# Two borders from attention to feed-forward: the order of LayerNorm, queries and transposes

## The chip, the cores and the metric

The kernel runs on one core of one Trainium2 chip. The time is the device time of one execution in microseconds (us). Engines are named as the profile names them: PE (TensorE), DVE (VectorE), ACT (ScalarE), POOL (GpSimd), SP (here the queue that issues every DMA). Each engine works through its own instructions in the order in which the program gives them; semaphores tie the engines together.

## The reference, cut to what matters

A network of four layers, attention A, feed-forward B, A, B, on one sequence of 2048 tokens of width 512, and the gradients of its input and of all weights. Every layer normalises its input without learned scale and is added back to it.

```python
def _A_ref(x, wqkv, wo):            # 32 heads of 16, linear attention
    q, k, v = split(x @ wqkv)
    phi = lambda t: jnp.where(t > 0, t + 1, jnp.exp(t)) + 1e-6
    pq, pk = phi(q), phi(k)
    kv = jnp.einsum("bhsd,bhse->bhde", pk, v)
    z = jnp.einsum("bhsd->bhd", pk)
    num = jnp.einsum("bhqd,bhde->bhqe", pq, kv)
    den = jnp.einsum("bhqd,bhd->bhq", pq, z)[..., None] + 1e-6
    return merge_heads(num / den) @ wo

def _B_ref(x, w_gate, w_up, w_down):
    return (sigmoid(x @ w_gate) * (x @ w_up)) @ w_down

x = x + _A_ref(_layernorm(x), A_wqkv, A_wo)      # layer 0
x = x + _B_ref(_layernorm(x), ...)               # layer 1
x = x + _A_ref(_layernorm(x), A_wqkv, A_wo)      # layer 2
x = x + _B_ref(_layernorm(x), ...)               # layer 3
# outputs: x and its vector-Jacobian product with grad_out
```

## The kernel before

The sequence is cut into 16 tiles of 128 tokens (`st`). The forward part takes about the first 430 us, the backward part the rest. All order is written out by hand: on each engine, instructions run as the Python emits them.

**Attention, `kq_fwd` (layers 0 and 2).** A loop over the 16 tiles projects keys and queries (`proj`, L604, four 128x512 matmuls each, in PSUM banks that rotate over "t", "t", "y"), takes the exponential on ACT (L621), and finishes phi on DVE with a clamp (L624) and `phi_out` (L627). The sum X = h^T phi(k) grows in four PSUM banks (L612); `X_some` emits XSTEP = 4 of its 64 matmuls per tile from tile 2 on. The queries of the last QLATE = 2 tiles, 14 and 15, are left for behind the loop: `late_q` emits the matmuls ("t_mm") and the exponential, and returns a function that does the clamp, `phi_out` and the store.

Behind the loop comes the border. X is copied out by ACT (L750), multiplied with the value weights (`kv_ps`, L758), masked (`kvbdT`, L760) and multiplied with wo (`M_ps`, L765); M turns normalised queries into the layer's output. For each tile, `prod` multiplies phi(q) by the sum z (DVE for tiles 0 and 1, POOL after that, L815), `front1` reduces it to the denominator (L821), `front2` adds epsilon, inverts and writes the normalised queries "pqn" (L831, L832, L833), `front3` transposes them on PE into the bank "ln" (L355) and copies them out on ACT (L364, "pqnT"). `attn_mm` multiplies by M (`y_ps`, L854), `attn_add` adds the residual (L862) and takes the LayerNorm statistics (bn_stats L448, aggregate L450 on DVE, three small POOL instructions L451, L452, L454). `ln.apply` normalises on ACT (L459), `stage_T` transposes that in the same bank "ln" and copies it out on DVE ("hT"). "ln" and "y" are single PSUM banks; "t", "g" and "u" have two buffers.

**Feed-forward, `ab_fwd` (layers 1 and 3).** For each tile, `gu` makes gate and up products of one of three column slices (L909, eight matmuls), two sigmoids on ACT (L911, L913), their product with up on DVE (`hh`, L914) and one more product on POOL (L915). `transposes(T, fs)` turns a slice around in a bank "t" (L923) and copies it out on ACT (L926). `finish` multiplies by w_down in bank "y" (L935) and adds on DVE (L937). The fronts of attention run FLAG = 3 tiles ahead inside this loop, so the first tile of feed-forward overlaps the last steps of the border. `fill` emits weight transposes, one group per "t" bank ("wT_ps", L390 in layer 1, L416 and L433 in layer 3); `fill.share` spreads the groups left evenly over the tiles left, and 16 groups are to be placed in layer 1, 34 in layer 3. `A.extra` holds the copy of a group whose transposes were emitted earlier. `early_T` transposes the first two tiles of the next attention layer, between layers 1 and 2.

The order that the change touches, before it, in the border:

```python
        A.front1(1)
        A.attn_y(0)
        A.front2(1)
        phis = [late_q(st) for st in range(NST - QLATE, NST)]
```

Of the kernel before, what the change touches and what calls it, by code (L numbers as in the profile page):

```python
# [23 lines left out]
NST = S // P  # L24
# [334 lines left out]
def evac_copy(k, dst, src, evac):  # L359
    nc = k.nc  # L360
    if evac == "vector":
        nc.vector.tensor_copy(dst, src)  # L362
    elif evac == "scalar":
        nc.scalar.copy(dst, src)  # L364
    else:
        nc.any.tensor_copy(dst, src)
# [183 lines left out]
XSTEP = 4  # L550
# [5 lines left out]
def kq_fwd(k, aq, l, ln, ln_next, x_src=None):  # L556
# [10 lines left out]
    with ExitStack() as ctx:  # L567
# [47 lines left out]
        def X_some(n, upto):  # L615
            while n > 0 and Xq and Xq[0][0] <= upto:
                X_mm(*Xq.pop(0))
                n -= 1
# [36 lines left out]
        def late_q(st):  # L655
            ps = proj(st, 0, ps_tile(k, "t", [P, D], F32, "t_mm"))
            e_t, a_t = qa_tiles()
            exp_to(e_t, ps)

            def phi():  # L660
                clamp(a_t, e_t)
                phi_out(A.pq_all[:, st, :], ps, a_t)
                save_phq(st, a_t)
            return phi
# [17 lines left out]
        for st in range(NST):  # L682
            if st == 2:
                X_ps += [ps_tile(k, "gu"[i % 2], [P, D], F32, "X_ps") for i in range(NDC)]
            both = st < NST - QLATE
            ps_k = proj(st, 1)
            if l == 0:
                e_t = work.tile([P, 2, D], BF16, name="e_t", bufs=2)
                a_t = work.tile([P, 2, D], BF16, name="a_t", bufs=3)
                ek, ak, eq, aqt = e_t[:, 0, :], a_t[:, 0, :], e_t[:, 1, :], a_t[:, 1, :]  # L690
            else:
                ek = work.tile([P, D], BF16, name="e_t", bufs=4)[:]
                ak = work.tile([P, D], BF16, name="ak_t", bufs=1)[:]
            exp_to(ek, ps_k)
            if l == 0 and st < 2:
                stage_hT([2 * st + 1], "scalar" if st else "vector")
            elif l == 2 and st == 0:
                stage_hT([2, 3], "vector")
            elif st % 2 == 1 and st >= 3:
                stage_hT([st + 1, st + 2], "vector" if l == 2 and st % 4 == 1 else "scalar")  # L700
            if l == 2 or not both:
                clamp(ak, ek)
                phi_out(pk_all[:, st, :], ps_k, ak)
            if both:
                ps_q = proj(st, 0, ps_tile(k, "u", [P, D], F32, "u_mm") if st == 1 else None)
                if l == 2:
                    eq, aqt = qa_tiles()
                exp_to(eq, ps_q)
            if l == 0:
                if st == 0:  # L710
                    stage_hT([2], "scalar")
                if st == 2:
                    ln.apply(4)
                if st != 1:
                    ln.apply(st + 3)
                if both:
                    clamp(a_t[:], e_t[:])
                    phi_out(pk_all[:, st, :], ps_k, ak)
            elif st in (1, 2):
                ln.apply(NST - 3 + st)  # L720
            if both:
                if l == 2:
                    clamp(aqt, eq)
                phi_out(A.pq_all[:, st, :], ps_q, aqt)
                save_phq(st, aqt)
            if l == 0:
                if st == 0:
                    ln.stats(4)
                ln.stats(st + 5)
            z_sum(st - ZLAG)  # L730
            store_pk(st)
            X_some(XSTEP, st - 2)

        z_ps = mm_tile()
        nc.tensor.matmul(z_ps[:], lhsT=k.ones32[:], rhs=zs, start=True, stop=False)
# [12 lines left out]
        for ic in range(NDC):  # L748
            X_mm(NST - 1, ic)
            nc.scalar.copy(X_sb[:, ic, :], X_ps[ic][:])  # L750
        nc.sync.dma_start(out=sv["X"].rearrange("(c p) j -> p c j", p=P), in_=X_sb[:])

        kv_ps = ps_tile(k, "y", [P, D], F32, "kv_ps")
        kv3 = kv_ps[:].rearrange("p (c f) -> p c f", c=NDC)
# [8 lines left out]
        for c in range(NDC):  # L763
            m_ps = ps_tile(k, "gu"[c % 2], [P, D], F32, "M_ps")
            nc.tensor.matmul(m_ps[:], lhsT=kvbdT[:, c, :], rhs=k.wo[:, c, :], start=True, stop=True)  # L765
            evac_copy(k, A.M_sb[:, c, :], m_ps[:], "vector" if c % 2 else "scalar")
        A.front1(1)
        A.attn_y(0)
        A.front2(1)
        phis = [late_q(st) for st in range(NST - QLATE, NST)]  # L770
        nc.scalar.activation(k.tab[:], k.neg[:], ACT.Sigmoid)
        mt_ps = []
        for jc in range(NDC):
            mt_ps.append(ps_tile(k, "gu"[jc % 2], [P, D], F32, "M_ps"))
            for c in range(NDC):
                nc.tensor.matmul(mt_ps[jc][:, c * P:(c + 1) * P], lhsT=k.wo[:, c, jc * P:(jc + 1) * P],
                                 rhs=kvbdT[:, c, :], start=True, stop=True)
        A.front3(1)
        phis[0]()
        A.ln.apply(0)  # L780
        for jc in range(NDC):
            nc.scalar.copy(MT_sb[:, jc, :], mt_ps[jc][:])
        nc.sync.dma_start(out=sv["MT"].rearrange("(c p) j -> p c j", p=P), in_=MT_sb[:])
        A.attn_mm(1)
        phis[1]()
    k.kv[l] = dict(kvbdT=kvbdT, zb=A.zb, rden_all=A.rden_all)

    def tail(fill):
        fill("tt", "vector")
        A.ln.stage_T(0)  # L790
        A.prod(2)
        A.prod(3)
        A.attn_add(1)
        A.front1(2)
        A.front2(2)
        A.extra = fill.mm("t")
    A.tail = tail
    return A
# [93 lines left out]
def ab_fwd(k, A, ln, fill, nxt=None, out_cb=None, last_cb=None):  # L892
# [3 lines left out]
    with ExitStack() as ctx:  # L896
# [20 lines left out]
        def transposes(T, fs):  # L917
            hh_t, hhT = T["hh"], T["hhT"]
            fcs = fchunks_of_slice(fs)
            tps = ps_tile(k, "t", [P, 8, P], BF16, "t_tp")  # L920
            for i, fc in enumerate(fcs):
                r = fc_rows(fc)
                nc.tensor.transpose(tps[0:r, i, :], hh_t[:, fc * P:fc * P + r], k.ident[:])  # L923
            nfull = len([fc for fc in fcs if fc_rows(fc) == P])
            if nfull > 0:
                nc.scalar.copy(hhT[:, fcs[0]:fcs[0] + nfull, :], tps[:, 0:nfull, :])  # L926
            if nfull < len(fcs):
                nc.scalar.copy(hhT[0:FLAST, NFC - 1, :], tps[0:FLAST, nfull, :])
# [21 lines left out]
        for st in range(NST):  # L950
            hT = ln.pop(st)
            T = dict(st=st,
                     ssd=wide.tile([P, 2, F], BF16, name="ssd_t"),
                     hh=wide.tile([P, F], BF16, name="hh_t"),
                     hhT=wide.tile([P, NFC, P], BF16, name="hhT"))
            nfill = fill.share(st)
            if st == 0:
                gu(T, hT, 0)
                A.extra("vector")
                A.front1(FLAG)  # L960
                A.front3(2)
                ln.apply(1)
                gu(T, hT, 1)
                transposes(T, 0)
                A.attn_y(2)
                ln.stage_T(1)
                gu(T, hT, 2)
                A.front2(FLAG)
            else:
                A.prod(st + FLAG)  # L970
                gu(T, hT, 0)
                if st == 1:
                    A.front3(FLAG)
                else:
                    A.attn_y(st + YLAG)
                after(st - 2)
                if nfill > 0:
                    fill("t", "vector")
                gu(T, hT, 1)
                if st == 1:  # L980
                    A.attn_y(FLAG)
                transposes(T, 0)
                ln.stage_T(st + 1)
                A.front1(st + FLAG)
                gu(T, hT, 2)
                A.front2(st + FLAG)
            if l == 1 and st == NST - 1:
                nc.scalar.activation(k.tab[:], k.neg[:], ACT.Exp)
            transposes(T, 1)
            ln.apply(st + YLAG)  # L990
            if st == NST - 1:
                if last_cb is not None:
                    last_cb(0)
                if nxt is not None:
                    nxt.early_T()
            if st == 0:
                fill("t", "vector")
            if prev is not None:
                finish(prev)
            if st > 0:  # L1000
                A.front3(st + FLAG)
            if st > 0 and nfill > 1:
                fill("t" * (nfill - 1), "scalar" if st % 2 else "vector")
            transposes(T, 2)
            nc.sync.dma_start(out=sv["ssd"][rows(st), :, :], in_=T["ssd"][:])
            nc.sync.dma_start(out=sv["hdd"][0, :, :, st, :].rearrange("g p w -> p g w"),
                              in_=T["hh"][:, 0:NG * GW].rearrange("p (g w) -> p g w", g=NG))
            nc.sync.dma_start(out=sv["hdl"][0, :, st, :], in_=T["hh"][:, NG * GW:F])
            prev = T
        if out_cb is not None:  # L1010
            out_cb(NST - 2)
        if last_cb is not None:
            last_cb(1)
        finish(prev)
        if out_cb is not None:
            out_cb(NST - 1)
# [747 lines left out]
```

## Time and profile before

| | |
|---|---|
| median of 3 runs | 1202.06 us (1201.79 to 1202.13) |
| the profiled execution | 1202.16 us |
| its span in the trace | 1200.4 us |
| PE busy in the span | 1169.6 us (97%) |
| DVE, ACT, POOL busy | 730.6, 593.2, 290.2 us |
| granted PE clock | 1.00 |
| DMA, mean | 213 GB/s |

A row of the timeline gives start and length in us, engine, line, operation, tiles (written <- read), shape and count; in brackets stands how long the engine had been idle before it and what ended that. Several instructions of one line in a row are merged ("x8"). A matmul's end is modelled, and the matmuls of a row overlap, so the idle time in brackets is a little shorter than the room that one more instruction would find. The list of waits adds up such idle time by who waited for whom. "issue" is time for which the profile shows no releaser. Lines are those of the code above.

### The profile page before, as it was taken

To read this page: it belongs to the slowest core of one execution; us is meant where nothing else is said; L and a number is where in the kernel's file an instruction comes from. 1 tells how busy PE (TensorE), PEld (TensorE's weight loads), DVE (VectorE), ACT (ScalarE), POOL (GpSimd) and SP (SyncE) were. 2 spreads that over 40 slices of the span, in tenths; PEclk is the share of its full clock that TensorE was granted. 3 is DMA by queue.
4 is the path that set the end of the run, shared out by engine and by line. 5 is a ranking of instruction groups with operands and counts; after the bars stand their busy time and mean duration, and the time that the engine had idled before them with its cause. 6 is when DMAs were issued, how large, how long until landed. Compare 5 with 4: busy or idle time off the path is not lost.

```text
span 1200.4 us, 21734 instructions
## 1 busy us (share of the span) xinstructions
PE 1169.6 (97%) x8185; PEld 717.5 (60%) x8302; DVE 730.6 (61%) x1414; ACT 593.2 (49%) x1100; POOL 290.2 (24%) x498
## 2 busy tenths in 40 slices
PE   8989999998999999999999999999999999999998
PEld 4445555444555555555546568865556745547887
DVE  6788886777777556665884760056664976751111
ACT  6667776547766644444635641144444625630010
POOL 5646665425666410000110010000100110110000
PEclk9999999999999999999999999999999999999999
DMA  8834455434546777977765859558897685749874
GB/s 263 290 136 156 168 180 183 154 137 165 188 149 232 237 228 249 336 217 222 239 190 165 263 172 315 136 161 261 256 298 224 207 275 164 231 117 350 258 208 151
DMA packets 266233, 256.05 MB, mean 213 GB/s; under 512 B 43280, under 2 KB 251024, under 8 KB 261264
## 3 DMA queue, kind: packets, MB, share of 16 engines
q1 hardware_dynamic: 266128, 254.65, 66.5%
q8 instruction: 65, 1.06, 0.4%
q14 instruction: 40, 0.33, 0.1%
HBM read 135.69 MB, written 118.92 MB: 212 GB/s over the span
## 4 chain that ended last, share of the span: by engine, by line
PE 92%; DVE 4%; ACT 2%; issue 1%; DMA 1%; another core or an unknown queue 0%; SPq 0%; ACTq 0%; DVEq 0%
PE p_ps L1408 17%; PE dh_ps L1174 13%; PE dh_ps L1622 7%; PE p_ps L1394 6%; PE dhh_ps L1059 6%; PE u_ps L909 6%; PE g_ps L909 6%; PE y_ps L935 6%; PE T_ps L1134 3%; PE GT_ps L1535 2%; PE y_ps L854 2%; PE dp_ps L1510 2%; PE dpk_ps L1653 2%; PE t_mm L604 2%; PE t_tp L923 2%; PE X_ps L612 1%
## 5 line engine op out<-in xcount | busy, mean ns | idle before, releaser
L1408 PE MATMUL p_ps<-p_set,p_a 128*128 128x256 bf16 (+1 forms) x2048 | 211.7, 264 | 0.6 <-DVE dw_stg L1384 0.5
L1408 PEld LDWEIGHTS <-p_a 128*128 128x128 bf16 x2048 | 185.9, 98 | 22.5 <-issue 0.7
L1067 DVE TENSOR_TENSOR dd<-dhh_ps,ssd 128x512 bf16<-128x512 f32 x144 | 82.5, 629 | 136.7 <-PE dhh_ps L1059 131.8
L1138 ACT COPY ddT<-T_ps 128x1024 bf16<-128x1024 bf16 (+1 forms) x96 | 83.0, 867 | 124.7 <-PE T_ps L1134 124.3
L1033 POOL TENSOR_SCALAR ab<-c 128x2 f32<-128x2 f32 x64 | 12.3, 192 | 436.4 <-DVE junk L1030 405.1
L915 POOL TENSOR_TENSOR ssd_t<-hh_t,oms 128x512 bf16<-128x512 bf16 (+1 forms) x96 | 101.7, 1064 | 55.5 <-ACT out_t L219 41.1
L1174 PEld LDWEIGHTS <-ddT 128*128 128x128 bf16 (+1 forms) x704 | 67.7, 98 | 69.3
L909 PEld LDWEIGHTS <-hT 128*128 128x128 bf16 x768 | 71.1, 98 | 56.6 <-DVE hT L362 1.0
L1384 DVE TENSOR_TENSOR dw_stg<-p_ps,dw_stg 128x512 bf16<-128x512 f32 (+3 forms) x44 | 28.5, 649 | 109.4 <-PE p_ps L1408 84.2
L909 PE MATMUL g_ps<-wg,hT 128*128 128x512 bf16 (+1 forms) x381 | 89.6, 357 | 0.8 <-DVE hT L362 0.6
L909 PE MATMUL u_ps<-wu,hT 128*128 128x512 bf16 (+1 forms) x384 | 90.0, 357 | 0.0
L914 DVE TENSOR_TENSOR hh_t<-u_ps,ssd_t 128x512 bf16<-128x512 f32 (+1 forms) x96 | 61.0, 636 | 45.9 <-PE u_ps L909 24.5
L1174 PE MATMUL dh_ps<-wgT,ddT 128*128 128x512 bf16 (+1 forms) x352 | 86.2, 379 | 0.0
L1174 PE MATMUL dh_ps<-wuT,ddT 128*128 128x512 bf16 (+1 forms) x351 | 81.2, 379 | 0.1
L1394 PE MATMUL p_ps<-p_a,p_set 128*128 128x512 bf16 (+1 forms) x343 | 79.9, 379 | 0.5
L1025 ACT ACTIVATE t_sb<-dh_ps,rstd_all 128x512 f32<-128x512 f32 x64 | 44.0, 687 | 71.2 <-issue 38.4
L1059 PE MATMUL dhh_ps<-wdT,gT 128*128 128x512 bf16 (+1 forms) x341 | 75.8, 355 | 2.1 <-DVE dd L1067 0.5
L935 PE MATMUL y_ps<-wd,hhT 128*128 128x512 bf16 (+1 forms) x322 | 75.1, 379 | 2.2 <-DVE x L937 0.6
L1030 DVE SCALAR_TENSOR_TENSOR junk<-t_sb,h_ld 128x512 bf16<-128x512 f32 x64 | 44.0, 688 | 48.7 <-ACT t_sb L1025 46.9
L911 ACT ACTIVATE ssd_t<-g_ps 128x512 bf16<-128x512 f32 (+1 forms) x96 | 53.2, 554 | 30.8 <-PE g_ps L909 30.6
L1386 ACT CAST dw_stg<-p_ps 128x512 bf16<-128x512 f32 (+2 forms) x43 | 24.1, 560 | 67.8 <-PE p_ps L1408 61.1
L1394 PEld LDWEIGHTS <-p_set 128*128 128x128 bf16 (+1 forms) x352 | 33.6, 100 | 34.9
(239 smaller groups left out, 2158.4 us busy)
## 6 DMA issues: line engine op xcount, KB each, us to landing
p_set<-sv_hdd SPq DMA_DIRECT2D x30, 1024.0 KB, 6.4
sv_ssd<-ssd_t SPq DMA_DIRECT2D x32, 688.0 KB, 3.4
ssd<-sv_ssd SPq DMA_DIRECT2D x24, 688.0 KB, 5.2
sv_hdd<-dd SPq DMA_DIRECT2D x48, 320.0 KB, 3.6
sv_hdd<-hh_t SPq DMA_DIRECT2D x32, 320.0 KB, 2.6
h_ld<-sv_h SPq DMA_DIRECT2D x32, 256.0 KB, 5.1
p_a<-sv_h SPq DMA_DIRECT2D x16, 512.0 KB, 6.2
p_set<-sv_dqk SPq DMA_DIRECT2D x8, 1024.0 KB, 7.9
```

The costliest lines, as they stand in the source:

```text
L909: nc.tensor.matmul(ps[:, 0:w], lhsT=hT[:, kc, :], rhs=w_sb[:, kc, c0:c0 + w], start=(kc == 0), stop=(kc == NDC - 1))
L911: nc.scalar.activation(ssd_t[:, 0, c0:c0 + w], g_ps[:, 0:w], ACT.Sigmoid)
L914: nc.vector.tensor_tensor(hh_t[:, c0:c0 + w], u_ps[:, 0:w], ssd_t[:, 0, c0:c0 + w], ALU.mult)
L915: nc.gpsimd.tensor_tensor(ssd_t[:, 1, c0:c0 + w], hh_t[:, c0:c0 + w], oms[:, 0:w], ALU.mult)
L935: nc.tensor.matmul(y_ps[:], lhsT=T["hhT"][0:r, fc, :], rhs=k.wd[0:r, fc, :], start=(fc == 0), stop=(fc == NFC - 1))
L1059: k.nc.tensor.matmul(ps[:, 0:w], lhsT=gT[:, jc, :], rhs=k.wdT[:, jc, c0:c0 + w], start=(jc == 0), stop=(jc == NDC - 1))
L1067: k.nc.vector.tensor_tensor(dd[:, a, c0:c0 + w], ps[:, 0:w], ssd[:, a, c0:c0 + w], ALU.mult)
L1138: nc.scalar.copy(ddT[:, :, f0:f0 + nfull, :], tps[:, :, 0:nfull, :])
L1174: nc.tensor.matmul(T["dh"][:], lhsT=ddT_block(T, a, fc), rhs=(k.wuT, k.wgT)[a][0:r, fc, :], start=(i == 0), stop=(i == 2 * NFC - 1))
L1394: nc.tensor.matmul(ps[0:r, :], lhsT=set_t[:, st, c * P:c * P + r], rhs=self.ops[j["l"], "g"][:, st, :], start=(st == 0), stop=(st == NST - 1))
L1408: nc.tensor.matmul(ps[:, icl * w:(icl + 1) * w], lhsT=self.ops[j["l"], "h"][:, st, ic * P:(ic + 1) * P], rhs=set_t[:, st, 0:w], start=(st ...
L1622: nc.tensor.matmul(dh_ps[:], lhsT=lhsT, rhs=rhs, start=(i == 0), stop=(i == len(ops) - 1))
```

## The change

In `kq_fwd`, behind the loop: the queries of tile 14 are projected ahead of `kv_ps` and not behind y(0); y(0) with its add and statistics stands ahead of `front1(1)`; `front3(1)` stands behind `ln.apply(0)`; `stage_T(0)` stands ahead of `attn_mm(1)`. `tail` keeps one weight-transpose group of three, and gives `front2(2)` to the feed-forward loop. In the first tile there, `front3(2)` and y(2) come one slice later, the extra group's copy goes to ACT, two fill groups stand where one stood, and the last transposes of tile 0 move into tile 1. One X matmul of tile 2 is left for later. `early_T` moves behind the last tile's transposes.

```diff
-            X_some(XSTEP, st - 2)
+            X_some(XSTEP - (st == 2), st - 2)
...
             nc.scalar.copy(X_sb[:, ic, :], X_ps[ic][:])
         nc.sync.dma_start(out=sv["X"].rearrange("(c p) j -> p c j", p=P), in_=X_sb[:])
+        phis = [late_q(NST - 2)]
...
+        A.attn_y(0)
         A.front1(1)
-        A.attn_y(0)
         A.front2(1)
-        phis = [late_q(st) for st in range(NST - QLATE, NST)]
+        phis.append(late_q(NST - 1))
         nc.scalar.activation(k.tab[:], k.neg[:], ACT.Sigmoid)
...
-        A.front3(1)
         phis[0]()
         A.ln.apply(0)
+        A.front3(1)
         for jc in range(NDC):
             nc.scalar.copy(MT_sb[:, jc, :], mt_ps[jc][:])
         nc.sync.dma_start(out=sv["MT"].rearrange("(c p) j -> p c j", p=P), in_=MT_sb[:])
+        A.ln.stage_T(0)
         A.attn_mm(1)
         phis[1]()
...
     def tail(fill):
-        fill("tt", "vector")
-        A.ln.stage_T(0)
         A.prod(2)
         A.prod(3)
         A.attn_add(1)
         A.front1(2)
-        A.front2(2)
         A.extra = fill.mm("t")
...
             if st == 0:
                 gu(T, hT, 0)
-                A.extra("vector")
-                A.front1(FLAG)
-                A.front3(2)
+                A.front2(2)
+                A.extra("scalar")
                 ln.apply(1)
                 gu(T, hT, 1)
                 transposes(T, 0)
-                A.attn_y(2)
+                A.front3(2)
                 ln.stage_T(1)
                 gu(T, hT, 2)
+                A.attn_y(2)
+                A.front1(FLAG)
                 A.front2(FLAG)
             else:
                 A.prod(st + FLAG)
                 gu(T, hT, 0)
                 if st == 1:
+                    transposes(prev, 2)
                     A.front3(FLAG)
...
-                if nxt is not None:
-                    nxt.early_T()
             if st == 0:
-                fill("t", "vector")
+                fill("tt", "vector")
             if prev is not None:
                 finish(prev)
...
-            transposes(T, 2)
+            if st > 0:
+                transposes(T, 2)
...
         if last_cb is not None:
             last_cb(1)
+        if nxt is not None:
+            nxt.early_T()
         finish(prev)
```

## The prediction

> **What bounds the kernel now.** I read the page's busy times, then the list of TensorE's waits, then the timeline of the borders, then the DVE and POOL rows inside them.
>
> ```profile
> PE 1169.6 (97%) x8185; PEld 717.5 (60%) x8302; DVE 730.6 (61%) x1414; ACT 593.2 (49%) x1100; POOL 290.2 (24%) x498
> ```
>
> PE is idle for 1200.4 - 1169.6 = 30.8 us in all; its work is not changed by the edit, only its order, so the time moves with its waits. The list of waits (us in total, times, longest):
>
> ```profile
> PE ln_tp L355 <- DVE pqnstage L833: 4.5, 6, 1.5
> PE y_ps L854 <- ACT pqnT L364: 2.3, 2, 1.3
> PE kv_ps L758 <- ACT X_sb L750: 2.2, 8, 0.3
> ...
> PE X_ps L612 <- DVE pq_all L627: 1.4, 1, 1.4
> PE t_tp L923 <- DVE hh_t L914: 1.2, 2, 0.6
> ```
>
> Most of them stand in two places, the border of layer 0 (57 to 80 us) and of layer 2 (262 to 285); in the view by windows PE is busy 17.18 and 17.11 of 23 us there, at a granted clock of 1.00. The timeline of the first one:
>
> ```profile
> 57.04 2.06 ACT L750 CAST X_sb<-X_ps 128x512 bf16<-128x512 f32 x4
> ...
> 58.17 0.22 PE L758 MATMUL kv_ps<-X_sb,wqkv 128*128 128x128 bf16 x1 [0.28 <-ACT X_sb L750]
> ...
> 63.02 1.89 PE L604 MATMUL t_mm<-wqkv,hTst 128*128 128x512 bf16 x8
> 63.26 0.68 DVE L862 TENSOR_TENSOR x<-y_ps,x_bf 128x512 f32<-128x512 f32 x1
> ...
> 66.19 0.40 PE L355 MATMUL ln_tp<-ident,pqnstage 128*128 128x128 bf16 x4 [0.39 <-DVE pqnstage L833]
> ...
> 70.08 1.04 PE L909 MATMUL g_ps<-wg,hT 128*128 128x512 bf16 x3 [0.28 <-DVE hT L362]
> ...
> 71.39 0.18 DVE L450 BATCH_NORM_AGGREGATE ln_mv<-ln_stats 128x2 f32<-128x6 f32 x1
> 71.48 0.65 DVE L821 TENSOR_REDUCE den<-prod 128x32 f32<-128x512 bf16 x1
> ...
> 72.17 0.18 DVE L831 TENSOR_SCALAR den<-den 128x32 f32<-128x32 f32 x1
> 72.39 0.35 DVE L832 RECIPROCAL rden_all<-den 128x32 f32<-128x32 f32 x1
> 72.64 0.26 POOL L454 TENSOR_SCALAR ln_nmr<-ln_mv,rstd_all 128x1 f32<-128x1 f32 x1
> 72.78 0.69 DVE L833 TENSOR_TENSOR pqnstage<-pq_all,rden_all 128x512 bf16<-128x512 bf16 x1
> ...
> 73.53 0.40 PE L355 MATMUL ln_tp<-ident,pqnstage 128*128 128x128 bf16 x4 [1.54 <-DVE pqnstage L833]
> ```
>
> The eight matmuls in 1.89 us give a pitch of 0.216 (one lasts 0.38); 128-column ones keep 0.056 (L776: 16 in 1.06). "Lost" below is the time beyond these pitches from start to start, a little more than the bracketed idle. Per border: before the kv products 0.46 + 3 x 0.43 = 1.77; before pqn of tile 1 0.54; from its transposes (66.19) to the first g_ps (70.08) 3.89 less 2.00 of work = 1.90; in feed-forward tile 0 1.71 (73.53) and 0.77 (79.21). Together 6.69; the same rows of layer 2 give 6.90.
>
> **The change, part by part.** *Queries of tile 14 ahead of the kv products.* Four matmuls (0.86) go to where PE waits for the X_sb copies, which come 0.49 apart from ACT and end at 59.10 whatever PE does. Their exp is queued behind the copies. Lost there: 1.77 falls to 0.95.
>
> *The same matmuls are missing after y(0).* PE's last y(0) slot ends at 63.02; what is left is 4 x 0.216 + 16 x 0.056 = 1.76, where 2.63 stood. And pqn(1) comes later: its reduce, which ran at 62.67 while DVE waited for y(0), now stands behind the add, the stats and the aggregate. From rows, start to start: add 0.72, stats 0.75, aggregate 0.09, reduce 0.70, den 0.22, reciprocal 0.39, pqn 0.69, 0.05 to PE: 3.61 from the add, against 2.93 now (63.26 to 66.19). So PE waits 63.26 + 3.61 - (63.02 + 1.76) = 2.09 where 0.54 stood. This is the price of putting the LayerNorm first on DVE.
>
> *From there to the first g_ps.* stage_T(0) now follows front3(1) at once, and both use the one bank "ln": 0.40 for the transposes, 0.03 to ACT, 0.58 for its copy, 0.05 back, less 0.23 of slots = 0.83 lost. y(1) and the one remaining fill (1.09) then cover the hT(0) copy (0.93 from the transposes); clamp and phi of tile 14 (0.29 and 0.69) stand ahead of it, and I find about 0.2 to spare. 1.90 becomes 0.83. LayerNorm's tile 0 is early: the first g_ps comes 2.38 after the transposes of pqn(1) instead of 3.89, partly because two fills (0.45) moved on.
>
> *Feed-forward tile 0.* front3(2) stands behind slices 0 and 1 and four transposes: PE gets there 3.46 + 0.23 + 0.12 (it waits for hh of slice 0) = 3.81 after the first g_ps. DVE: clamp and phi of tile 15 now come after the hT(0) copy, which ends 0.2 ahead of g_ps: -0.2 + 0.29 + 0.57 put the add of x(1) at about +0.66. From start to start: to the stats 0.73, aggregate 0.74, reduce 0.10, hh of slice 0 0.60 (before, it was behind pqn), den 0.61, reciprocal 0.22, pqn 0.40: +4.06. That hh starts at +2.83, POOL's product of the slice 0.82 later (as 73.39 to 74.21), and lasts 1.15: from +3.65 to +4.80. A pqn that meets a running POOL product waits for it:
>
> ```profile
> 87.24 0.85 POOL L915 TENSOR_TENSOR ssd_t<-hh_t,oms 128x352 bf16<-128x352 bf16 x1
> ...
> 87.60 1.04 DVE L833 TENSOR_TENSOR pqnstage<-pq_all,rden_all 128x512 bf16<-128x512 bf16 x1
> ```
>
> POOL ends at 88.09, DVE at 88.64: a wait, then 0.55 of work. So pqn(2) ends at 4.80 + 0.55 = +5.35, PE goes on at +5.40 and loses 1.59. The ACT copy of that pqnT then stands behind the hhT copy: 1.14 less 0.23 = 0.91 lost before stage_T(1). After it slice 2, y(2), transposes, and two fills on the two banks "t": the second waits for ACT's hhT copy, 0.39 + 0.05 + 0.58 + 0.05 - 0.45 = 0.62. In tile 1 the moved last transposes of tile 0 need a third "t" bank, which the first fill's copy on DVE frees; it is queued behind the add, stats, reduce and pqn(3): 3.52 + 0.40 after the add of x(2), which follows y(2) by 0.2, while PE brings 0.22 + 0.22 + 0.62 + 0.22 + 1.73 = 3.01: 1.14 lost. Tile 0: 0.12 + 1.59 + 0.91 + 0.62 + 1.14 = 4.38 against 2.48.
>
> One border is then 0.95 + 2.09 + 0.83 + 4.38 = 8.25: **+1.56** at layer 0 and **+1.35** at layer 2.
>
> *One X matmul less at tile 2.* It moves behind the loop (0.22). In layer 0 it stood at the 1.4 us wait for pq_all; the loop gains nothing, since the next queries wait for pk_all of tile 2 at 18.62 (t_mm at 18.68) on DVE anyway: +0.22. In layer 2 PE does not wait there: 0.
>
> *early_T behind the transposes.* Its eight matmuls (0.45) now fill the wait of the last y_ps:
>
> ```profile
> 216.35 2.54 PE L935 MATMUL y_ps<-wd,hhT 128*128 128x512 bf16 x11 [0.61 <-DVE x L937]
> ```
>
> Lost 0.77 becomes 0.32: **-0.45**. Its two copies and hT stores come later; the copies follow the aggregate of tile 14 (217.06) with 0.33 and 0.41, and the first user is the t_mm at 218.72: covered by some 0.8.
>
> *Fills.* The border takes three instead of four. With 13 left in layer 0, tile 3 takes one; with 31 left in layer 2, the shares are 2 a tile and 3 in the last. PE's work is the same, but there the last transposes need a third "t" bank behind two fills, freed by an ACT copy: again **+0.62**. SP's order shifts by a few stores (phq, pqn, hT, wT, 0.4 to 1 us of issue each); their tiles are next written some tiles later, and no row of PE's waits names a DMA there: 0.
>
> Sum: 1.56 + 1.35 + 0.22 - 0.45 + 0.62 = 3.30. The profiled execution took 1202.16 (span 1200.4), 0.10 above the median of 1202.06: **1205.5 us**. Nothing behind gives it back: after 430 us the list of PE's waits holds 3.0 us in 770, none for a DMA.
>
> **The rivals.** *Port lost (to 1209.1).* At pqn(1) and pqn(3), POOL has prod of a later tile ready right behind ln_nmr. By rows, from the aggregate pqn starts at 72.78 - 71.39 = 1.39 and a POOL product could start at 72.64 + 0.22 - 71.39 = 1.47 (79.70 stands 0.22 behind its ln_nmr). I take pqn first, by 0.08. If POOL wins, pqn waits most of 1.15: about 0.9 at two places of two borders, +3.6. The Trainium skill ("SBUF — State Buffer", Who interferes with whom) says that a tensor_tensor with two SBUF inputs and a GpSimd op that reads SBUF exclude each other, whichever starts first; the two rows above agree, and by it this case is all or nothing.
>
> *Not slower (1200.0 to 1202.3).* The DVE queue of tile 0 is shorter than I count. Before, pqn(2) ended 73.47 - 70.08 = 3.39 after the first g_ps; at that pace the 3.81 of moved PE work would cover it. Then 1.59 goes at each border, 3.30 - 3.18 = +0.1, and with the fill's copy also in time (1.14 each) -2.2. It decides at pqn(2) ending 3.8 after g_ps. Against it: 0.6 (hh), 0.8 (clamp and phi) and 0.5 (POOL), all rows now ahead of it.
>
> *Clock (about 1212).* PE now stands 2.09 and 0.83 almost together; the largest wait so far is 1.7 and the clock stayed at 1.00. If it fell to half for the next 3.4 us of work, each border would lose 3.4, +6.8. The Trainium skill ("TensorE: Matmul & The Clock Gate", What's actually happening) lets it fall to half after an idle window of about 3.4 us; by that rule 2.1 is not enough, and no row here shows a fall.
>
> *The change does not bring tile 0 forward:* no; 2.38 against 3.89 is in the order itself.
>
> **How the numbers follow.** Forecast 0.70 (1203.6 to 1207.0: 0.5 either way for each border's queue order, and 0.6 for the last fill); port lost 0.12 (whole or half, to 1209.3); not slower 0.14; clock 0.02; the rest 0.02. The range 1203.6 to 1209.3 leaves out 0.18. A measurement of this kernel can tell about 0.2% (2.4 us) from no change: above 1204.46 lie the port, the clock and most of the forecast, 0.75; between 1199.66 and 1204.46 lie the rest of the forecast and most of the not-slower case, 0.20; below 0.05.
>
> **What would show it.** Right: ln_tp <- pqnstage grows from 4.5 us to about 7; the kv waits halve in number; new PE waits appear on ACT pqnT for ln_tp, and on evacuated "t" banks for t_tp and wT_ps; the wait of 0.61 at the last y_ps halves. Wrong: front3(2) without a wait, DVE evacuating the first fill before pqn(3), or pqn rows of 0.9 and more behind POOL's prod at tile 1.

## The result and the profile after

The change makes the kernel slower: median 1207.3 us (1206.46 to 1208.34, 6 runs) against 1202.31 (1201.79 to 1203.14, 6 runs), a ratio of 1.0041 [1.0029, 1.0052]. The profiled execution took 1206.46 us, span 1204.7, which is 4.30 above the profiled one of before; the forecast was 3.30 above it, and a range of 1203.6 to 1209.3.

The page's line of busy times, and the head of the list of PE's waits (us in total, times, longest):

```profile
PE 1178.5 (98%) x8302; PEld 718.6 (60%) x8302; DVE 731.4 (61%) x1411; ACT 594.9 (49%) x1103; POOL 291.1 (24%) x498
```

```profile
PE ln_tp L355 <- DVE pqnstage L832: 6.0, 6, 1.9
PE ln_tp L355 <- ACT pqnT L364: 2.7, 4, 0.7
...
PE kv_ps L759 <- ACT X_sb L750: 1.1, 4, 0.3
PE t_tp L922 <- DVE wdT L362: 1.0, 1, 1.0
```

These are the signs that the forecast named: the kv waits are halved in number (8 to 4), ln_tp <- pqnstage grew from 4.5 to 6.0 (7 was forecast), ln_tp now also waits for ACT's pqnT, and t_tp waits for evacuated "t" banks (the row shown is layer 3's; layer 1 has its like, and the last tile one of 0.5), and the wait at the last y_ps fell from 0.6 to 0.2. PE's idle time fell all the same, from 30.8 to 1204.7 - 1178.5 = 26.2 us. A busy PE is not the same as a PE at work: something made its instructions longer. The timeline of the first border, all engines, shows where:

```profile
66.07 0.69 DVE L832 TENSOR_TENSOR pqnstage<-pq_all,rden_all 128x512 bf16<-128x512 bf16 x1
66.15 2.78 POOL L814 TENSOR_TENSOR prod<-pq_all,zb 128x512 bf16<-128x512 bf16 x2
...
66.82 0.40 PE L355 MATMUL ln_tp<-ident,pqnstage 128*128 128x128 bf16 x4 [1.95 <-DVE pqnstage L832]
...
68.27 1.91 PE L853 MATMUL y_ps<-M_sb,pqnT 128*128 128x512 bf16 x4
...
73.54 1.15 POOL L914 TENSOR_TENSOR ssd_t<-hh_t,oms 128x512 bf16<-128x512 bf16 x1 [0.28 <-ACT wt_st L364]
73.91 1.33 DVE L832 TENSOR_TENSOR pqnstage<-pq_all,rden_all 128x512 bf16<-128x512 bf16 x1
...
75.29 0.40 PE L355 MATMUL ln_tp<-ident,pqnstage 128*128 128x128 bf16 x4 [0.73 <-DVE pqnstage L832]
```

The four y(1) matmuls take 1.91 us where four of this shape take 1.03 elsewhere: half speed. The view by windows (length, busy time of PE, PEld, DVE, ACT, POOL, then the granted clock, DMA share and GB/s) confirms it, over each border and then over 3.41 us on either side of each change of the clock's records:

```profile
57.00:80.00 23.00, 17.39 (x123) 9.75 (x122) 18.37 (x34) 15.39 (x29) 8.00 (x11) 0.93 0.26 90
262.00:290.00 28.00, 21.44 (x139) 11.25 (x138) 20.96 (x42) 16.88 (x31) 10.00 (x15) 0.94 0.36 123
```

```profile
64.21:67.62 3.41, 1.06 (x16) 0.81 (x14) 3.21 (x7) 3.07 (x5) 2.48 (x4) 1.00 0.00 0
67.62:71.03 3.41, 3.14 (x14) 1.69 (x14) 3.00 (x7) 2.18 (x5) 1.31 (x2) 0.50 0.50 176
272.43:275.84 3.41, 1.26 (x11) 0.83 (x12) 3.27 (x7) 3.16 (x7) 3.30 (x4) 1.00 0.22 79
275.84:279.25 3.41, 3.41 (x13) 1.45 (x12) 3.16 (x7) 1.66 (x5) 0.72 (x3) 0.50 0.62 211
```

The records read 0.5 from 67.62 to 71.03 and from 275.84 to 279.25, 3.41 us each time, right behind a stretch in which PE was busy for 1.06 and 1.26 of 3.41 us. In before's profile the records read 1.00 through both borders. So the waits that the forecast counted are there, and beside them a fall of the clock at each border, a rival that had been given 0.02.

To weigh the parts without the noise of a whole run I compare stretches between two instructions. These repeat to about 0.05 us where the code is the same; "border 0" and "border 2" go from the mask on kv (`kvbdT`) to the last add of feed-forward tile 0:

| stretch, us | before | after | forecast change | measured |
|---|---|---|---|---|
| copy of z to `kvbdT`, both layers | 3.52 | 3.52 | 0.04 | 0.00 |
| border 0 | 28.49 | 30.38 | +1.30 | +1.89 |
| border 2 | 28.66 | 30.68 | +1.07 | +2.02 |
| adds of tiles 13 to 14, layer 1 (early_T) | 8.34 | 7.89 | -0.45 | -0.45 |
| adds of tiles 14 to 15, layer 3 (last fills) | 4.50 | 5.33 | +0.84 | +0.83 |
| all behind that, to DVE's last instruction | 769.32 | 769.30 | 0 | -0.02 |

(The forecast's 1.56 and 1.35 a border, less the 0.22 of a fill that leaves it and the 0.04 of the first row, 0.06 at layer 2. The copy of z itself starts at 56.55 and 56.49, and anywhere from 56.14 to 57.34 in the kernels below.) All that was not forecast, 0.59 and 0.95, lies inside the two borders. What lies between these stretches differs by 0.08 in layer 1 and by 0.01 elsewhere.

### The profile page after: what moved, and what is told of

Its sections match the earlier page's. It is cut to its first block, busy times and chain, and to the rows that moved or that the text cites. A ratio compares the mean times of both kernels' runs of the same rounds, so it can differ in the third digit from the quotient of the medians.

```text
span 1204.7 us, 21854 instructions
## 1 busy us (share of the span) xinstructions
PE 1178.5 (98%) x8302; PEld 718.6 (60%) x8302; DVE 731.4 (61%) x1411; ACT 594.9 (49%) x1103; POOL 291.1 (24%) x498
## 3 DMA queue, kind: packets, MB, share of 16 engines
q8 instruction: 65, 1.06, 0.4%
## 4 chain that ended last, share of the span: by engine, by line
PE 93%; DVE 4%; ACT 2%; DMA 1%; issue 1%; POOL 0%; DVEq 0%; ACTq 0%
PE p_ps L1410 17%; PE dh_ps L1176 13%; PE dh_ps L1624 7%; PE p_ps L1396 6%; PE dhh_ps L1061 6%; PE g_ps L908 6%; PE y_ps L934 6%; PE u_ps L908 6%; PE T_ps L1136 3%; PE y_ps L853 2%; PE dpk_ps L1655 2%; PE GT_ps L1537 2%; PE dp_ps L1512 2%; PE t_mm L604 2%; PE X_ps L612 2%; PE t_tp L922 2%
## 5 line engine op out<-in xcount | busy, mean ns | idle before, releaser
L1061 PE MATMUL dhh_ps<-wdT,gT 128*128 128x512 bf16 x372 | 82.5, 357 | 0.5 <-DVE dd L1069 0.5
L934 PE MATMUL y_ps<-wd,hhT 128*128 128x512 bf16 (+1 forms) x352 | 81.3, 379 | 0.2 <-DVE x L936 0.2
```

The costliest lines, as they stand in the source:

```text
L934: nc.tensor.matmul(y_ps[:], lhsT=T["hhT"][0:r, fc, :], rhs=k.wd[0:r, fc, :], start=(fc == 0), stop=(fc == NFC - 1))
L1061: k.nc.tensor.matmul(ps[:, 0:w], lhsT=gT[:, jc, :], rhs=k.wdT[:, jc, c0:c0 + w], start=(jc == 0), stop=(jc == NDC - 1))
```

## Experiments

The theory: waits as forecast, +2.9 in these stretches, and the clock costs the rest. The rival: waits that were not counted.

**Keeping PE busy.** e1 fills the long wait with matmuls that write a free bank and are read by nobody:

```diff
+        busy_ps = ps_tile(k, "y", [P, D], F32, "busy_ps")
+        for i in range(8):
+            nc.tensor.matmul(busy_ps[:], lhsT=k.wo[:, 0, 0:P], rhs=k.wo[:, 0, :], start=True, stop=True)
         A.front3(1)
```

> The changed kernel with eight 128x512 matmuls (8 x 0.216 = 1.73 us) into the free bank y, ahead of front3(1); nobody reads them, so they add work that the reference does not have. They stand in the 2.1 us in which PE waits for pqn(1) at both borders. Theory A (the waits cost what the prediction says, 3.3 us, and the rest is PE at half clock for 3.41 us at each border): the clock stays at 1.00, the two borders lose their slow windows, about 0.5 each, and the time falls by 0.8 to 1.3 us against the changed kernel, although work was added. Theory B (the half clock lies beside waits and costs nothing; the rest is some other wait): the clock may stay up, but the time does not move by more than 0.2 us. By either, the wait for pqn(2) in the first feed-forward tile is 0.9 with the half clock and 1.6 without it.

Measured: 1206.63 us, ratio to before 1.0035 [1.0021, 1.0048]. Border 0 fell to 29.74 with the clock at 1.00; there the wait for pqn(1) left 0.38 and the next wait, for pqn(2), grew from 0.89 to 1.65. At border 2 the fall came later, at 283.29, behind a stretch with 1.34 us of PE work around that second wait, and the border took 31.15. The 0.8 to 1.3 us that were expected did not come: one border gained 0.64 and the other lost 0.47. So the fall follows the thin stretch, not the particular wait. e8 therefore fills both:

```diff
                 transposes(T, 0)
+                more_ps = ps_tile(k, "y", [P, D], F32, "more_ps")
+                for i in range(5):
+                    nc.tensor.matmul(more_ps[:], lhsT=k.wo[:, 0, 0:P], rhs=k.wo[:, 0, :], start=True, stop=True)
                 A.front3(2)
```

> The kernel after with matmuls that nobody reads in two waits of each border: 8 of 512 columns ahead of the transposes of pqn of tile 1 (1.73 us of the 2.1 there) and 5 ahead of those of pqn of tile 2 (1.08 of the 0.9 to 1.65 there). Theory (the excess over the forecast is the clock, 0.6 in layer 0 and 0.95 in layer 2): the granted clock is 1.00 at both borders, the stretch from the kv products to the add of feed-forward tile 0 is 29.7 in layer 0 and about 29.9 in layer 2 (30.38 and 30.68 in after), and the time is 1.3 under after, near the 1205.5 of the forecast. Rival (the excess are waits that were not counted): the stretches stay at 30.4 and 30.7 whatever the clock does, or grow by the added work.

Measured: 1205.52 us, 1.0023 [1.0014, 1.0032]; all ten runs show a clock of 1.000; borders 29.75 and 29.83. By windows and in the timeline of e8:

```profile
57.00:80.00 23.00, 19.24 (x135) 10.38 (x137) 18.70 (x36) 15.45 (x29) 8.01 (x11) 1.00 0.28 98
262.00:290.00 28.00, 23.29 (x161) 12.50 (x163) 22.01 (x43) 18.15 (x35) 10.80 (x16) 1.00 0.40 133
```

```profile
68.22 1.03 PE L856 MATMUL y_ps<-M_sb,pqnT 128*128 128x512 bf16 x4
...
74.73 0.40 PE L355 MATMUL ln_tp<-ident,pqnstage 128*128 128x128 bf16 x4 [0.40 <-DVE pqnstage L835]
```

More work made the kernel 0.63 and 0.85 us a border faster, and brought the borders to +1.26 and +1.17 over before, against +1.30 and +1.07 forecast. The rival falls: with the clock held, each border comes within 0.1 us of its forecast. From start to start the second row lost 0.57 behind five added matmuls of 0.216: a wait of 1.65 without them, where 1.59 was forecast.

**The reduce of tile 1 first again.** e2 exchanges two calls of after, to price "LayerNorm first on DVE":

```diff
-        A.attn_y(0)
         A.front1(1)
+        A.attn_y(0)
```

> The changed kernel with front1(1), the reduce of tile 1, ahead of attn_y(0) again, as before the change: one DVE instruction moved back. Theory A: the wait for pqn(1) falls from 2.1 to about 1.4 at each border (1.1 to 1.4 us for both), and if the clock then stays at 1.00 another 0.8 to 1.3 us: 1.9 to 2.7 in all. If the clock still falls: 1.1 to 1.4 alone. Theory B (the wait for pqn(1) is set by something else than the reduce behind the LayerNorm, for one by ACT's table load): no change.

Measured: 1205.66 us, 1.0025 [1.0015, 1.0035]; the borders are only 0.13 and 0.18 shorter than after's. The wait for pqn(1) fell from 2.11 to 1.42 as the reduce came forward. The next row gave most of it back; the timeline of e2:

```profile
66.98 0.40 PE L355 MATMUL ln_tp<-ident,pqnstage 128*128 128x128 bf16 x4 [1.26 <-DVE pqnstage L832]
68.55 0.59 PE L355 MATMUL ln_tp<-ident,hstage 128*128 128x128 bf16 x4 [1.18 <-ACT pqnT L364]
```

Here pqnT's copy on ACT stands behind `ln.apply(0)`, which waits for POOL's ln_nmr, now later: 0.84 lost became 1.34. And the clock fell at both borders as before. I had counted DVE's queue and not ACT's, so what was expected of this kernel did not come. The median lies 1.6 under after's all the same: the profiled run (1207.15) has a mean clock of 0.997, as all of after's have, but six of the eight runs have 0.998 or 0.999.

**The small terms.** e3 takes after and puts one more fill group into tile 2 of layer 3, so that the last tile has two:

```diff
-                    fill("t", "vector")
+                    fill("tt" if st == 2 and nfill > 1 else "t", "vector")
```

> The changed kernel with one more weight-transpose group in tile 2 of the second feed-forward layer, ahead of its column slice 1, so that the last tile has two groups again and not three. Theory A: the wait of 0.6 us for an ACT copy of bank t in the last tile goes and nothing comes in tile 2: 0.6 us less. Theory B (the last tile is bound by its y_ps chain and the wait is covered): no change.

Measured: 1206.46 us, 1.0032 [1.002, 1.0045]. The last two adds came 4.50 apart again (-0.83: 0.61 of wait, 0.22 of work), and tile 2 took 0.36 more. Net -0.5: the third "t" bank was the cost.

e4 is before with the two edits outside the borders, early_T behind the last transposes and one X matmul later:

```diff
-            X_some(XSTEP, st - 2)
+            X_some(XSTEP - (st == 2), st - 2)
...
-                if nxt is not None:
-                    nxt.early_T()
...
+        if nxt is not None:
+            nxt.early_T()
         finish(prev)
```

> The kernel before with two parts of the change alone: early_T behind the last tile's transposes, and one X matmul less in tile 2. The two show at different places of the trace. early_T: the wait of PE before the last y_ps falls from 0.8 to 0.3 start to start, 0.45 us less at the first query of layer 2. X matmul, by the prediction: the M products of layer 0 come 0.22 later; by the rival (the trace of the change has them 0.06 earlier): at the same time within 0.1. In all 0.2 to 0.5 us less than before.

Measured: 1202.33 us, 0.9998 [0.9989, 1.0007]; adds 13 to 14 took 7.90 (-0.44), and the borders kept their lengths. The X matmul is the other part: from the phi of tile 12's keys (DVE, L627) to the copy of z, layer 0 took 8.80 where before takes 8.58. Together that is -0.22; in a whole run it does not show, in the stretches it does.

**Two by two: the part ahead of the feed-forward, and tile 0.** e5 is after with tile 0 in before's order:

```diff
                 gu(T, hT, 0)
-                A.front2(2)
-                A.extra("scalar")
+                A.extra("vector")
+                A.front1(FLAG)
+                A.front3(2)
                 ln.apply(1)
...
-                A.front3(2)
+                A.attn_y(2)
...
-                A.attn_y(2)
-                A.front1(FLAG)
                 A.front2(FLAG)
```

(and `front2(2)` back in `tail`, `transposes(T, 2)` back in tile 0.)

> The kernel after with feed-forward tile 0 of the border in the order of before (last reduce and pqn of the flagged tile first, queries' transposes of tile 2 right behind slice 0, last transposes of the tile inside tile 0); the part ahead of the feed-forward, the early queries of tile 14 and the early_T call stay as in after. If the new order of tile 0 is itself the loss (the prediction's terms: 4.38 of waits against 2.48), taking it back returns about 1.9 us at each border, and the time falls to about 1202.7. If the loss is set by the DVE chain that begins with y(0), so that pqn(2) comes when it comes (before it ended 3.39 after the first g_ps, and g_ps is now 1.5 earlier), PE meets the same wait at another place: by the traced durations put into that order the waits of tile 0 grow by about 0.3 a border, and the time is 1206.5 to 1207.5. Whether the clock falls is then seen in its records: the theory of thin work says that it falls at both borders again.

Measured: 1207.8 us, 1.0041 [1.0028, 1.0053], borders 31.70 and 31.79. Undoing half of the change made the borders 1.3 and 1.1 longer, where +0.3 was expected. The timeline of e5:

```profile
73.16 0.57 PE L355 MATMUL ln_tp<-ident,pqnstage 128*128 128x128 bf16 x4 [2.60 <-DVE pqnstage L833]
73.52 1.92 PE L909 MATMUL g_ps<-wg,hT 128*128 128x512 bf16 x4
```

The wait for pqn(2) stands right behind slice 0, as that theory said, and the clock falls (73.23 to 76.64) where PE has nothing but dense work: the eight matmuls of this slice at about twice their pitch, some 8 x 0.21 = 1.7 us, the most that 3.41 us at half clock can cost. Without it the border would be near 30.0 by this estimate, 0.3 over e8's, or more where part of the slow time hid in a wait.

e9 is before with the new tile 0 alone (the hunks of the diff inside the feed-forward's first tile, `front2(2)` and `transposes(T, 2)` moved with it, the fills as before).

> The kernel before with the new order of feed-forward tile 0 alone: pqn of tile 2 behind the hh of slice 0, the queries' transposes of tile 2 behind those of hh, the flagged reduce last, the last transposes of the tile in tile 1. The part ahead of the feed-forward, the four fills and early_T stay as before. With after and the kernel that has the new front alone it makes a square of two by two. If the losses of the two parts add (the forecast's terms: 4.38 against 2.48 in tile 0, less than nothing ahead of it), each border loses 1.9 and the time is 3.8 over before, 1206.3. If the front sets what tile 0 can lose (before, the first g_ps is 1.5 later, so that pqn of tile 2 and the flagged pqn on DVE have that much more time), each border loses 0.7 to 1.1, and the time is 1204.0 to 1205.0. The clock should stay at 1.00, since the 2.1 us wait for pqn of tile 1 is not there.

Measured: 1204.15 us, 1.0016 [1.0007, 1.0025], borders 29.41 and 29.46: +0.92 and +0.80, with the clock at 1.00 in the profile. The two parts do not add. With the clock's cost out, tile 0 alone costs 0.9, the new front alone about 1.5 (30.0 - 28.49), both together 1.26: given the new front, the new tile 0 is the better of the two, since it moves work of PE ahead of the late pqn(2).

**One edit alone.** e6 is before with the queries of tile 14 ahead of the kv products:

```diff
+        phis = [late_q(NST - 2)]
         kv_ps = ps_tile(k, "y", [P, D], F32, "kv_ps")
...
-        phis = [late_q(st) for st in range(NST - QLATE, NST)]
+        phis.append(late_q(NST - 1))
```

> The kernel before with one edit: the queries of tile 14 ahead of the kv products. The waits for the copies of X fall by 0.82 at each border (1.77 to 0.95) in both theories. Theory: the four matmuls are then missing behind y(0), where the chain on DVE sets when pqn of tile 1 comes, so that wait grows from 0.54 to about 1.4 and the time stays within 0.4 of before. Rival: the work is moved into a wait and nothing is late for it, and both borders gain 0.82, so that the time is about 1.6 under before.

Measured: 1201.91 us, 0.9997 [0.9988, 1.0006]; borders 28.18 and 28.28 (-0.31, -0.38). The wait for pqn(1) grew from 0.56 to 1.42, the whole 0.86 of the moved work; the profit is the wait for y(1) (1.16 to 0.84), not the kv waits. Theory, not rival, though the gain of 0.69 at the two borders is more than the 0.4 that the theory allowed. Eight of the eleven runs have a mean clock below 1.000, so a part of it is lost again.

**A better order.** e7 keeps before's front and the moved early_T of e4 (the X edit, which the expectation names as well, is not in it), and gives tile 0 an order by what is ready:

```diff
                 A.extra("vector")
                 A.front1(FLAG)
-                A.front3(2)
                 ln.apply(1)
                 gu(T, hT, 1)
-                transposes(T, 0)
-                A.attn_y(2)
-                ln.stage_T(1)
+                A.front3(2)
                 gu(T, hT, 2)
+                transposes(T, 0)
+                A.attn_y(2)
+                ln.stage_T(1)
                 A.front2(FLAG)
```

> A third order, on the base of before: the queries' transposes of tile 2 stand behind slice 1 of feed-forward tile 0, the flagged pqn ahead of the LayerNorm of tile 1, the transposes of hh behind slice 2, and the two edits that cost nothing or gained (early_T behind the last transposes, one X matmul later) are kept. From before's rows: pqn(2) ends 3.39 after the first g_ps, and slices 0 and 1 with the fill put PE there 3.5 to 3.9 after it, so the waits of 1.54 (layer 0) and its like in layer 2 go, the waits of 0.6 to 0.8 for the t bank stay; with early_T's 0.45 the time is about 2.0 under before, 1200.0 to 1200.8. Rival: the waits come back at the ln bank or at y(2), as they did in after, and the time is within 0.5 of before. The clock should stay at 1.00, since no wait is longer than those of before.

Measured: 1200.6 us, 0.9985 [0.9976, 0.9993]. In its list of waits ln_tp <- pqnstage fell from 4.5 to 1.5: the losses of 1.71 for pqn(2) are gone. Part of them is given back at the first g_ps of tile 1, which loses 0.76 (0.98 by its rows, of which 0.22 is the place of a matmul whose record is missing; the 0.22 of before is such a place too), and a little later (0.36 and 0.64): borders -0.68 and -0.42, and -0.45 at early_T.

e10 adds e6's edit to e7:

> The third order of tile 0 (e7) and the early queries of tile 14 (e6) together. Each gained where it was tried alone, e6 0.31 and 0.38 at the borders, and they touch different waits (kv products and y(1) by the one, pqn of tile 2 by the other): if they add, the stretches from the kv products to the add of feed-forward tile 0 are 27.50 and 27.86 (28.49 and 28.66 in before), and the time is 0.7 under e7. Rival: the earlier g_ps brings back a wait for pqn of tile 2, whose DVE chain does not come earlier, and the stretches are those of e7, or the 1.4 us wait thins the work enough for the clock to fall and they are longer.

Measured: 1200.58 us, 0.9984 [0.9975, 0.9993]: nothing over e7. The rival had the reason: in the profiled run the clock fell at both borders (28.49 and 29.06). It did not fall in every run. The five runs with a mean clock of 1.000 took 1199.63 to 1200.23, the three at 0.999 took 1200.58 to 1200.72, the three at 0.997 took 1201.84 to 1202.25: by the medians about 0.6 and 1.8 us for one fall and for two.

e11 is e10 with one call later, the flagged pqn behind the copy of the last fill:

```diff
                 ln.stage_T(1)
-                A.front2(FLAG)
...
             if st == 0:
                 fill("t", "vector")
+                A.front2(FLAG)
```

> As the kernel with both, with the flagged pqn of DVE behind the copy of the last fill of tile 0. That kernel's base (e7) still lost 0.98 at the first g_ps of tile 1, which waited for the hh of a slice behind the reciprocal and pqn of the flagged tile on DVE, and 0.61 for a t bank. If that queue on DVE is the cause, the 0.98 falls by 0.2 or more at each border and the time is 0.4 to 1.0 under that kernel. Rival: pqn of the flagged tile is then late for its own transposes in tile 1, and the time is the same or longer.

Measured: 1199.75 us, 0.9975 [0.9966, 0.9984]; borders 27.18 and 27.22. The expected time came, and not by the expected way: the first g_ps of tile 1 loses 0.75, as in e10 (0.76), waiting for the hT copy behind the add and the statistics. Gone is what stood behind it, 0.36 at y(3) of border 0 and 0.63 at a fill's bank of border 2. Both were late on ACT behind `ln.apply(2)`, which waits for POOL's ln_nmr. The timelines of e10 and e11 there:

```profile
79.15 0.69 DVE L834 TENSOR_TENSOR pqnstage<-pq_all,rden_all 128x512 bf16<-128x512 bf16 x1
79.41 0.57 POOL L454 TENSOR_SCALAR ln_nmr<-ln_mv,rstd_all 128x1 f32<-128x1 f32 x1
```

```profile
78.30 0.27 POOL L454 TENSOR_SCALAR ln_nmr<-ln_mv,rstd_all 128x1 f32<-128x1 f32 x1
78.38 0.72 DVE L834 TENSOR_TENSOR pqnstage<-pq_all,rden_all 128x512 bf16<-128x512 bf16 x1
```

In e10 ln_nmr meets DVE's pqn and takes 0.57; in e11 it runs ahead of it and takes 0.27, and `ln.apply(2)` starts 1.01 behind that g_ps and not 1.31. The front of e11 is that of e10, so the two profiles show one order at two phases of the clock's grid. Windows of e10, then of e11:

```profile
64.03:67.44 3.41, 1.48 (x19) 0.90 (x16) 3.17 (x9) 2.95 (x5) 2.50 (x5) 1.00 0.19 67
67.44:70.85 3.41, 3.32 (x21) 2.18 (x20) 2.50 (x6) 2.13 (x5) 0.94 (x1) 0.50 0.32 113
```

```profile
65.17:68.58 3.41, 2.12 (x20) 1.38 (x21) 3.10 (x7) 2.96 (x7) 2.98 (x4) 1.00 0.44 154
```

In e10 the thin stretch falls into one window of the grid, which then holds 1.48 us of PE's time, and the next runs at half clock; in e11 the grid lies 1.1 later, the same stretch is split, no window at either border holds less than 2.12, and nothing falls.

e12 is e11 with five unread matmuls ahead of `front3(1)`, as in e1.

> The kernel of e11 with five more matmuls of 512 columns that nobody reads (1.08 us) in the 1.42 us wait ahead of the transposes of pqn of tile 1. Of e10, which has the same order up to the feed-forward, the five runs with a clock of 1.000 took 1199.63 to 1200.23 and the three with 0.997 took 1201.84 to 1202.25; of e11 four ran at 1.000 (1198.45 to 1199.75) and seven at less. If it is thin work in one of the clock's windows that brings the fall, and the place of the windows differs from run to run, then the filled wait keeps the clock at 1.000 in all runs, nothing is late for the added matmuls, and the median falls to that of e11's runs at 1.000: 1198.4 to 1199.4. Rival: the clock falls as often as in e11, or the matmuls delay the transposes, and the median stays at 1199.7 or above.

Measured: **1198.89 us** (1198.4 to 1199.58), 0.9967 [0.9955, 0.9979]; all six runs at 1.000, where seven of e11's eleven were below, borders 27.18 and 27.23 as in e11, so nothing is late for the added matmuls. It beats both kernels: 3.9 us under before.

## Why the prediction was right, and where it was not

*Direction and range: right, mostly for its own reasons.* In before to after, from the copy of z to the end, the profiles differ by 4.36 us; with the clock held (e8) by 2.87. The forecast for that part was 3.08, the 3.30 less the 0.22 of X, which lies ahead of it. Most of the difference of 0.2 is the fill that moves into layer 1's later tiles: tile 2 took 0.22 more for it and tile 3 0.22 less. That the range held is in part luck: the measured 1207.3 lies above the forecast's own 1203.6 to 1207.0, in the part that was put there for the port, and the clock took it there.

*A slip in the base.* The 6.90 of layer 2 counts as lost some 0.27 in which a y(1) matmul and a weight transpose run whose records are missing (the rows at 273.44 and 274.99 have three of four). Without it layer 2 gives 6.63, its border +1.62 and the sum 3.57; with the clock held (e8) that border's forecast would be +1.34 where +1.17 was measured.

*Queries of tile 14; pqn(1).* 0.95 at the kv products was 0.87, and 2.09 at pqn(1) was 2.11 and 2.04. That the LayerNorm ahead of the reduce delays pqn(1) is shown by e2, where exchanging them takes 0.69 off the wait, and that the moved matmuls are missing there by e6, where the wait grows by exactly their 0.86.

*Bank "ln".* 0.83 was 0.84 at both borders.

*Tile 0.* With the clock held: hh of slice 0 cost a wait of 0.09 for 0.12, pqn(2) 1.65 for 1.59, ACT's copy 0.88 for 0.91, second fill 0.61 for 0.62, last transposes 1.12 for 1.14. In after itself pqn(2) lost only 0.89, because PE came there later.

*Port.* The narrow case went as taken: pqn(1) started at 66.07 and POOL's product at 66.15, the 0.08 that was worked out, and pqn kept its 0.69; pqn(2), behind a POOL product that ended at 73.54 + 1.15 = 74.69, ended at 75.24, 0.55 later, as forecast. By the rule of the Trainium skill cited there ("SBUF — State Buffer", Who interferes with whom), this was to be all or nothing; the two rows agree. What the forecast did not see is that the clamp of tile 14, behind pqn(1), now met POOL's product: it took 1.24 (66.68), where the next one took 0.28. In e8, with the clock held, the hT(0) copy all the same ended (69.08) ahead of the first g_ps (69.30), so PE lost nothing by it.

*early_T and the last fill.* -0.45 and +0.62 were -0.45 and +0.61 (e3, e4). *X, +0.22 in layer 0:* right. The start of the border varies by more than that between kernels with the same code, but the end of the loop does not: from the phi of tile 12's keys to the copy of z it takes 8.58 or 8.59 in all seven profiles with before's X order and 8.79 or 8.80 in all seven with the new one. The loop ahead gave nothing back (tiles 4 to 12 took 24.2 to 24.5 in both groups), and in layer 2 both take 40.71 or 40.72 from the first phi to the copy, as forecast.

*The step that failed: the clock.* "The largest wait so far is 1.7 and the clock stayed at 1.00 ... 2.1 is not enough" judged by the length of one wait. What decides, as the windows show, is how little PE does in a window of 3.41 us: the waits of 2.1 and 0.84, almost together, left 1.06 and 1.26 of work. The base was also luckier than I knew: its profiled run had no fall at a border (its thinnest window held 1.80), but of the runs of before that shared a chip with e9 to e11, 17 of 27 had a mean clock of 1.000 (median 1202.66) and 10 had less (1202.7 to 1204.23). All six of after had 0.997.

*The rival's price failed too.* "Each border would lose 3.4" doubles the work of a whole 3.4 us; but 3.41 us at half clock can lose 1.7 at most, as in e5. At border 0 PE's rows lose 1.5 in the slow window, and 0.76 of that came back at pqn(2), for which PE would have waited, and 0.13 at the two small waits around it: 0.6, and 0.63 was measured. At border 2 PE had work in the whole window and lost 1.7: the same sum gives 0.8 to 0.9, and 0.85 was measured.

By the page cited there (the Trainium skill, "TensorE: Matmul & The Clock Gate", What's actually happening), the clock falls after an idle window of about 3.4 us, in windows that run freely and do not start with the kernel. The free-running windows agree with e10 and e11; "idle" read as "without work" does not, since windows with 0.81 to 1.54 us of work brought a fall here, and the measurement decides.

## What to carry to other kernels

When an order is changed, count PE's work in every stretch of 3.4 us around the waits, not the length of the longest wait; where it gets below about 1.6 us, compare the granted clock and the length of a known matmul, and read a PE that is "busier" and slower as a clock that fell. A wait that can't be removed can be filled with matmuls that nobody reads: that was worth 1.5 us in after (e8) and 0.9 in e11 (e12). And when a chain on DVE sets the end, moving PE's work ahead of it only moves the wait (e6); what pays is to put PE's ready work between the chain's start and its end (e7).

## What the runs showed of the hardware

The changes of the granted clock lie on a grid of 3.4133 us: in after's profile the second fall (275.84) and one at the very end (1204.26) begin 61 and 333 steps behind the first (67.62). The grid's place against the program differs from run to run, so the same kernel has runs with no fall, one and two, as in e10.

The threshold lies a little under half a window. In fourteen profiles, with the windows laid on the clock's own records, the eleven windows inside the run that brought a fall held 0.81 to 1.54 us of PE's busy time, the one at the end of each run 1.04 or less, and every window that brought none, from the first record of the full clock on, held 1.57 or more. The two that come closest, of e10 (with a fall) and of e5 (without):

```profile
268.83:272.24 3.41, 1.54 (x22) 1.19 (x21) 3.24 (x9) 2.80 (x5) 2.11 (x4) 1.00 0.08 28
62.99:66.40 3.41, 1.57 (x20) 1.07 (x17) 3.17 (x8) 2.57 (x4) 1.57 (x4) 1.00 0.02 5
```

Some matmul records are missing, and one of 512 columns is worth 0.22, so the exact point stays open. Nor did I try whether short matmuls or transposes count for less than 512-column ones.
